# Four products of the first feed-forward block written ahead of a pair's scales

## The chip, the cores and the metric

One core of a Trainium2 chip runs the kernel. The metric is the device time of one execution in microseconds; for several runs the median is given. Beside it stands one profiled execution, from which all rows below come.

## The reference

Attention in which a query sees only the keys of its own cluster, and then a feed-forward block with a maximum of three products. Inputs: q, k, v of 4 batches x 8 heads x 768 tokens x 64, centroids of 8 heads x 16 x 64, three weights of 512 x 768 and one of 768 x 512.

```python
q_assign = np.argmax(np.einsum('bhsd,hcd->bhsc', q_n, c_n), axis=-1)
k_assign = np.argmax(np.einsum('bhsd,hcd->bhsc', k_n, c_n), axis=-1)
mask = q_assign[:, :, :, None] == k_assign[:, :, None, :]
scores = np.where(mask, scale * np.matmul(q, k.transpose(0, 1, 3, 2)), -1e9)
attn = softmax(scores)
x = np.matmul(attn, v)            # then tokens x 512
h = np.maximum(np.maximum(x @ w1, x @ w2), x @ w3)
out = h @ w_out
```

## The kernel before

Attention goes by heads, 32 in all, counted through the batches (head 8 is the first of batch 1), and by pairs of heads: pair (1,1) is the second pair of batch 1, heads 10 and 11. The tokens of a head are sorted by cluster. For each pair, `load_rows` (L591) loads rows of q, k and v into one of five `rows` buffers each; `sums` (L603 on ScalarE, L607 on VectorE) takes squares and the largest value; `scales` makes powers of two from them: small operations (L614 to L618), three matmuls that spread them over the partitions into a buffer called `one` (L623), a reduction (L628), a reciprocal (L631). `split_kv` and `split_q` (L657, L671 on ScalarE, L658, L672 on VectorE) write each row as two half-precision numbers. `scatter` (L692, GpSimd) sends key and value rows to their sorted places in memory, `read_back` fetches them in order (L727, L730). `order_q` sorts the queries with one-hot matrices (L747 on VectorE, L749 on TensorE). `scores` is matmuls (L784 to L791), a maximum (L795), exponentials (L800) and two half-precision parts (L804, L805), which a DMA transposes; `values` (L825 to L830) multiplies them with v, into a `one` buffer. Outputs go back to token order by a gather (L848) and are split and transposed for the feed-forward block (`x_split`); the last two heads of batch 0 are turned by matmuls on the spot instead (`turn`, L874 to L887).

The feed-forward block of a batch has 36 first products and 6 second ones. A first product (`hidden(jt, i)`) is twelve matmuls (L940) into a `one` buffer and one evacuation: a copy on ScalarE for i = 0 (L950), a running maximum on VectorE for i = 1, 2 (L952). After i = 2 a cast on ScalarE (L956) and a subtraction on VectorE (L957) make the two parts of h. In batch 0 the products of the two halves of the tokens alternate by three: products 0 to 2 are those of the first half with the first 128 columns, products 3 to 5 those of the second half. The first 9 matmuls of a product need x of pairs 0 to 2, the last three that of pair 3, which `turn` of head 7 finishes. The second products (`outp`, L973) take h and the output weights. The weights of products 18 to 35 are loaded and converted meanwhile (L287, then L292 on ScalarE, L294 on VectorE).

Two things set the order of the work. `put(at, p, u)` notes that piece u is written down in round `at`, at place p within it; rounds go by heads. The same p becomes the priority of its instructions (`at_prio`): the kernel is built with a scheduler that lays out the instructions of every engine ahead of time, each as soon as it can go, the lower p first. Buffers of one name, however, go round in the order in which the pieces are written down: there are two `one` buffers (`ps_one`), shared by `scales`, `values`, `hidden`, `outp` and a step of the weight scales (L257). `when(p, k)` moves pieces of batch 1 on by up to 2 heads, so `scales` of pair (1,1) stands at 7.6 in round 8, that of pair (1,2) at 9.1 in round 9, and `turn` of head 7 at 7.55 in round 8. `spread` puts the 42 units of batch 0's block evenly between 9.05 and 16: product 0 at 9.05 in round 9, product 1 at 9.2, then one every 0.165. `values` of head 8 ends round 9, behind product 5.

Of the kernel before, what the change touches and what calls it, by code (L numbers as in the profile page):

```python
# [23 lines left out]
def sorted_attn__then__maxout_ffn(  # L24
# [18 lines left out]
    B, H, D, S = qk.shape  # L43
# [724 lines left out]
    def turned(b, h):  # L768
        return b == 0 and h >= H - 2
# [138 lines left out]
    def split_after(b, pr):  # L908
        k = b * H + 2 * pr + 5
        return k if pr < NPAIR - 2 and k < B * H else None  # L910
# [98 lines left out]
        verdict.append(nc.values_load(bad, min_val=0, max_val=1))  # L1009


    plan = {}

    def put(at, p, u, *args):
        plan.setdefault(int(at), []).append((p, u, args))

    def spread(units, first, last, late=0):
        for i, u in enumerate(units):
            k = first + i * (last - first) / len(units)
            put(min(max(k, 0), B * H), k + late, u)  # L1020


    AHEAD = 2.0

    def when(p, k):
        return p + AHEAD * max(0.0, 1.0 - (k - H) / H) if k >= H else p

    for i in range(NRING):
        put(0, -4.95 + 0.01 * i, clear_ring, i)
    for b in range(B):  # L1030
        for hf in range(2):
            k = b * H + 4 * hf
# [9 lines left out]
        for pr in range(NPAIR):  # L1042
            u = pair_units(b, pr)
            k = b * H + 2 * pr
# [9 lines left out]
            for h in range(2):  # L1054
                put(max(k + h - 4, at), when(k + h - 3.85, k), u["split_kv"][h])
                at, p = max(k + h - 2, 0), when(k + h - 2.5, k)
                if H <= k + h < H + 4:
                    at, p = H + 1, max(p, H + 0.7)
                put(at, p, u["scatter"][h])
                for n, x in enumerate(u["read"][h]):  # L1060
                    p = when(k + h - 1.5, k) if not n or k + h >= H else k + h - 0.95
# [3 lines left out]
    for b in range(B):  # L1065
        for h in range(H):
            k = b * H + h
            put(H + 1 if k == H else k, when(k, k), scores, b, h)
            put(k + 1, when(k + 0.5, k) if k >= H - 1 else k + 1.2, values, b, h)
            if turned(b, h):  # L1070
                put(3, 3.5 + 0.1 * h, token_places, b, h)
                put(k + 1, k + 1.25 if k < H - 1 else when(k + 0.55, k), turn, b, h)
            else:
                put(min(k + 1 + LATE + (k + 5 < H), B * H), when(k + 0.6 + LATE + (k + 5 < H), k), gather, b, h)
        put(b * H + 3, b * H + 2.6, x_scale, b)
        for pr in range(NPAIR):
            k = split_after(b, pr)
            if turned(b, 2 * pr):
                continue
            if not b and pr == 2:  # L1080
                put(H - 1, H - 0.7, x_split, b, pr)
            elif k is not None:
                put(k + 2 * (not (b or pr)), when(k, k) + 0.01, x_split, b, pr)
            else:
                k = b * H + 2 * pr + 2 + LATE
                if k <= B * H:
                    put(k, when(k - 0.35, k - 1 - LATE), x_split, b, pr)
        if b + 1 < B:
            k = b * H + H + LATE
            units = [ffn_units(b, gi) for gi in range(NG)]  # L1090
            hid = [x[: 3 * JT] for x in units]
            if b:
                hid = [u for x in hid for u in x]
            else:
                hid = [u for jt in range(JT) for x in hid for u in x[3 * jt : 3 * jt + 3]]
            units = hid + [u for x in units for u in x[3 * JT :]]
            spread(units, k + 0.05, k + H, 0)
    put(B * H, B * H - 0.5, judge)
    spread(w_units(range(JT // 2)), 1, 6, 1)
    spread(w_units(range(JT // 2, JT)), 9, 11.5, 0)  # L1100
    spread(wo_units(), 11.5, 14, 0)

    def at_prio(p, u, *args):
        tc.cur_priority = 100000 + int(p * 1000)
        u(*args)

    at_prio(-12, lambda: centroids(load_centroids()))
    for k in range(B * H + 1):
        for p, u, a in sorted(plan.pop(k, []), key=lambda x: x[0]):
            at_prio(p, u, *a)  # L1110
    assert not plan, sorted(plan)
    at_prio(B * H, x_split, B - 1, NPAIR - 1)
    for gi in range(NG):
        for u in ffn_units(B - 1, gi):
# [745 lines left out]
```

## Time and profile before

| | |
|---|---|
| median of three runs | 754.81 us (749.6 to 756.33) |
| profiled execution | 751.73 us, span of its instructions 750.0 us |
| TensorE matmuls busy | 620.3 us, 83% of the span |
| VectorE busy | 489.4 us, 65% |
| ScalarE busy | 419.8 us, 56% |
| GpSimd busy | 407.7 us, 54% |
| mean granted TensorE clock | 0.917 |

Shares over the whole span say little here, since the limits change on the way: the attention of batch 0 alone until some 165 us, then attention with feed-forward blocks between, and the last block alone from 647 us on. The rows below therefore go by stretches and by the time line around 165 to 212 us. In a time line an entry has its start and its length in us; an "idle" in brackets is the time its engine had nothing to run just before it, and what ended that.

### The profile page before, as it was taken

What the parts mean: (1) busy time and instruction counts of PE and PEld (TensorE: products, weight loads), DVE (VectorE), ACT (ScalarE), POOL (GpSimd) and SP (SyncE); (2) the same over time, 40 slices, a digit from 0 to 9 for tenths busy, and PEclk for the clock granted to TensorE, in tenths of its full rate; (3) what the DMA queues carried; (4) which work ended last, traced back from release to release, by engine and by line L of the source; (5) the groups of instructions that cost most, each with busy time, mean ns of one, the idle gap of its engine ahead of it and who ended that gap; (6) DMA issues with size and microseconds to landing.
All of it is one profiled execution on the core that took longest, in us unless ns stands there. A gap on an engine that the chain in (4) does not pass through costs nothing.

```text
span 750.0 us, 12895 instructions
## 1 busy us (share of the span) xinstructions
PE 620.3 (83%) x4333; PEld 336.3 (45%) x4333; DVE 489.4 (65%) x1229; ACT 419.8 (56%) x1011; POOL 407.7 (54%) x426
## 2 busy tenths in 40 slices
PE   3556466467889887799999989979989999999995
PEld 1223233233445453354455545534545654564552
DVE  5898867779888999896769787835565522121230
ACT  5348978725879775665758577735556512211111
POOL 4576677735553777576755787746657545000000
PEclk8677777568899999999999999999999999999998
DMA  8865998799894995598776668576536644200001
GB/s 321 280 179 129 263 199 174 149 245 341 211 314 94 243 311 124 128 228 187 171 145 177 125 161 158 134 160 155 130 80 146 131 89 115 69 1 29 15 1 46
DMA packets 226907, 119.22 MB, mean 159 GB/s; under 512 B 196560, under 2 KB 205776, under 8 KB 226832
## 3 DMA queue, kind: packets, MB, share of 16 engines
q1 hardware_dynamic: 214928, 99.80, 54.3%
q0 software_dynamic: 11904, 18.50, 9.2%
q8 instruction: 36, 0.59, 0.3%
q14 instruction: 39, 0.32, 0.1%
HBM read 58.36 MB, written 28.84 MB: 116 GB/s over the span
## 4 chain that ended last, share of the span: by engine, by line
PE 46%; DMA 15%; DVE 12%; ACT 10%; issue 8%; POOL 6%; SPq 1%; DVEq 0%; POOLq 0%; ACTq 0%
PE one L940 24%; PE one L973 12%; PE big L749 4%; POOL kv L692 4%; DMA pt<-hl 4%; ACT e L800 3%; POOL xb L848 3%; DMA rows<-in_v_dram 2%; DMA xb<-o,cl_idx 2%; DVE hot L747 2%; DMA rows<-in_kr_dram 2%; DMA kv<-kv,cl_idx 2%; DVE kv L658 1%; DMA o<-of 1%; PE big L788 1%
## 5 line engine op out<-in xcount | busy, mean ns | idle before, releaser
L940 PE MATMUL one<-x,w 128*128 128x384 f16 x1728 | 296.5, 328 | 9.1 <-ACT wf_h L950 3.7
L692 POOL DMA_INDIRECT kv<-kv,cl_idx x192 | 207.0, 1078 | 116.1 <-issue 55.2
L848 POOL DMA_INDIRECT xb<-o,cl_idx x180 | 191.4, 1063 | 114.7 <-DMA o<-of 59.6
L940 PEld LDWEIGHTS <-w 128*128 128x128 f16 x1728 | 167.7, 98 | 123.7 <-issue 15.3
L749 PE MATMUL big<-hot,q 128*128 128x512 f16 x384 | 113.4, 410 | 31.6 <-DVE hot L747 19.3
L800 ACT ACTIVATE e<-big,nm,sc_al 128x128 f32<-128x128 f32 x256 | 113.4, 462 | 42.2 <-DVE nm L796 27.4
L747 DVE TENSOR_SCALAR hot<-line,cl_code 128x1024 f16<-128x1024 f16 x192 | 93.0, 504 | 8.3 <-PE big L749 8.1
L749 PEld LDWEIGHTS <-q 128*128 128x128 f16 x384 | 36.6, 102 | 76.8 <-issue 47.3
L952 DVE SCALAR_TENSOR_TENSOR wf_h<-one,wf_h 128x384 f32<-128x384 f32 x48 | 26.5, 552 | 54.0 <-PE one L940 53.9
L952 DVE SCALAR_TENSOR_TENSOR vf_h<-one,vf_h 128x384 f32<-128x384 f32 x48 | 26.5, 552 | 46.5 <-PE one L940 42.8
L973 PE MATMUL one<-wo,vf_h 128*128 128x512 f16 x216 | 49.8, 387 | 7.0 <-ACT o L982 6.4
L800 ACT ACTIVATION_READ_ACCUMULATOR e<-big,nm,sc_al 128x1 f32 x256 | 53.6, 209 | 0.0
L973 PE MATMUL one<-wo,wf_h 128*128 128x512 f16 x216 | 48.6, 379 | 1.4 <-ACT o L982 1.4
L825 PE MATMUL one<-vt,pt 128*128 128x64 f16 x256 | 29.2, 202 | 16.0 <-DMA pt<-hl 14.9
L757 ACT CAST qt<-big 128x1024 f16<-128x1024 f32 x32 | 32.3, 1010 | 17.7 <-PE big L749 17.3
L805 DVE SCALAR_TENSOR_TENSOR hl<-e,hl 128x1024 f16<-128x1024 f32 x32 | 39.0, 1218 | 3.3 <-ACT hl L804 3.1
L982 ACT ACTIVATE o<-one,so 128x512 f32<-128x512 f32 x24 | 16.1, 683 | 43.3 <-PE one L973 41.1
L795 DVE TENSOR_REDUCE nm<-big 128x8 f32<-128x1024 f32 x32 | 38.9, 1215 | 1.8 <-PE big L791 1.7
L658 DVE SCALAR_TENSOR_TENSOR kv<-rows,sc_s,kv 128x384 f16<-128x384 f32 x64 | 37.3, 612 | 3.3 <-ACT kv L657 3.1
L956 ACT CAST wf_h<-wf_h 128x384 f16<-128x384 f32 x24 | 12.3, 514 | 48.0 <-DVE wf_h L952 47.9
L956 ACT CAST vf_h<-vf_h 128x384 f16<-128x384 f32 x24 | 12.3, 513 | 43.6 <-DVE vf_h L952 43.6
L657 ACT ACTIVATE kv<-rows,sc_s 128x384 f16<-128x384 f32 x64 | 35.7, 610 | 1.6 <-DVE sc_s L631 1.5
(242 smaller groups left out, 925.6 us busy)
## 6 DMA issues: line engine op xcount, KB each, us to landing
stage<-in_qk_dram SPq DMA_DIRECT2D x32, 384.0 KB, 7.2
wd<-in_moe_w_dram SPq DMA_DIRECT2D x18, 512.0 KB, 5.7
vt<-kv SPq DMA_DIRECT2D x32, 256.0 KB, 3.7
o<-of SPq DMA_DIRECT2D x30, 256.0 KB, 3.5
rows<-in_qr_dram SPq DMA_DIRECT2D x16, 384.0 KB, 5.2
rows<-in_kr_dram SPq DMA_DIRECT2D x16, 384.0 KB
rows<-in_v_dram SPq DMA_DIRECT2D x16, 384.0 KB, 3.4
out_dram<-o SPq DMA_DIRECT2D x24, 256.0 KB, 2.8
```

The lines of the kernel that those rows point to most:

```text
L657: d["kv_hi", h] = nc.scalar.activation(kv[:, :, at], x, AF.Copy, scale=s[:, i : i + 1])
L658: d["kv_lo", h] = nc.vector.scalar_tensor_tensor(kv[:, :, at + 1], x, s[:, i : i + 1], kv[:, :, at], op0=ALU.mult, op1=ALU.subtract)
L692: i = nc.gpsimd.indirect_dma_start(out=ring[at], out_offset=bass.IndirectOffsetOnAxis(ap=index(h, n, 1), axis=0), in_=d["kv", h][:, n].rea ...
L747: nc.vector.tensor_scalar(a, line, code, None, op0=ALU.is_equal)
L749: nc.tensor.matmul(t[:, lo : lo + 512], d["q16"][:, h * QT + n].rearrange("p a d -> p (a d)"), a[:, lo : lo + 512], start=(n == 0), stop=( ...
L795: d["max", i] = nc.vector.tensor_reduce(nm, ts, axis=AX.X, op=ALU.max)
L800: nc.scalar.activation(x[:, j], ts[:, j], AF.Exp, bias=nm[:, j : j + 1], scale=d["al"], accum_out=sm[:, j : j + 1])
L805: d["lo", i] = nc.vector.scalar_tensor_tensor(hl[:, 1], x, 2.0**14, hl[:, 0], op0=ALU.mult, op1=ALU.subtract)
L848: d["back", i] = nc.gpsimd.indirect_dma_start(out=d["x"][:, n, i * D : i * D + D], out_offset=None, in_=od, in_offset=bass.IndirectOffsetO ...
L940: nc.tensor.matmul(t[:, 0:NB], w16[:, jt, wa, i, ct], x16[b, ct][:, xa * QT + gi * G : xa * QT + (gi + 1) * G, :], start=(n == 0), stop=(n ...
L952: nc.vector.scalar_tensor_tensor(m, t[:, 0:NB], 2.0**-23, ms[jt], op0=ALU.mult, op1=ALU.max)
L973: nc.tensor.matmul(t[:, 0:DM], h16[jt][:, ha, tt * P : (tt + 1) * P], wo16[:, jt, wa, :], start=(n == 0), stop=(n == 3 * JT - 1),)
```

## The change

The first four units of batch 0's block, products 0 to 3, are written down in round 8 at 7.56, right behind `turn` of head 7 (7.55) and ahead of `scales` of pair (1,1) (7.6). Their priorities stay 9.05 and up, since they are called through `at_prio` with the p of the place they had. The other 38 units keep place and priority. `at_prio` itself only moves up in the file.

```diff
+    def at_prio(p, u, *args):
+        tc.cur_priority = 100000 + int(p * 1000)
+        u(*args)
+
     plan = {}
@@
     AHEAD = 2.0
+    NFIRST = 4
@@
             units = hid + [u for x in units for u in x[3 * JT :]]
-            spread(units, k + 0.05, k + H, 0)
+            if b:
+                spread(units, k + 0.05, k + H, 0)
+            else:
+                p0, n_units = k + 0.05, len(units)
+                p_unit = (H - 0.05) / n_units
+                for i in range(NFIRST):
+                    put(H, H - 0.44 + 0.001 * i, at_prio, p0 + i * p_unit, units[i])
+                spread(units[NFIRST:], p0 + NFIRST * p_unit, k + H, 0)
@@
-    def at_prio(p, u, *args):
-        tc.cur_priority = 100000 + int(p * 1000)
-        u(*args)
```

## Rows read from the trace of the kernel before

**Rows 1.** Busy time by stretches: us busy (instructions), then TensorE's clock, DMA.

```profile
172.00:194.00 22.00, 14.77 (x83) 6.39 (x79) 19.11 (x51) 12.96 (x32) 15.92 (x16) 0.72 1.07 340
194.00:212.00 18.00, 17.22 (x117) 9.33 (x116) 17.43 (x45) 11.31 (x19) 10.89 (x10) 0.96 0.83 242
212.00:342.00 130.00, 109.24 (x854) 61.46 (x853) 119.43 (x340) 97.57 (x244) 83.89 (x78) 0.97 0.75 197
342.00:743.00 401.00, 383.17 (x2642) 212.36 (x2640) 202.61 (x444) 186.11 (x458) 191.25 (x181) 1.00 0.50 111
```

**Rows 2.** Time line of TensorE, 168 to 195 us: start, us, instruction, [idle before].

```profile
168.64 1.62 PE L940 MATMUL one<-x,w 128*128 128x384 f16 x9
...
171.01 0.65 PE L940 MATMUL one<-x,w 128*128 128x384 f16 x3
...
193.59 0.48 PE L623 MATMUL one<-ident,sc 128*128 128x128 bf16 x3
193.86 1.49 PE L940 MATMUL one<-x,w 128*128 128x384 f16 x4
```

**Rows 3.** Time line of TensorE, 202 to 212 us.

```profile
202.21 2.11 PE L940 MATMUL one<-x,w 128*128 128x384 f16 x12 [0.78 <-DVE vf_h L952]
...
206.54 4.08 PE L940 MATMUL one<-x,w 128*128 128x384 f16 x24
...
211.97 0.19 PE L825 MATMUL one<-vt,pt 128*128 128x64 f16 x1
```

**Rows 4.** Time line of VectorE (DVE), 166 to 193 us.

```profile
166.66 0.56 DVE L628 TENSOR_REDUCE pall<-one 128x3 f32<-128x384 f32 x1
...
167.66 0.18 DVE L631 RECIPROCAL sc_s<-pall 128x3 f32<-128x3 f32 x1
...
172.61 0.61 DVE L658 SCALAR_TENSOR_TENSOR kv<-rows,sc_s,kv 128x384 f16<-128x384 f32 x1
...
175.03 1.01 DVE L672 SCALAR_TENSOR_TENSOR q<-rows,sc_s,q 128x768 f16<-128x768 f32 x1
...
183.21 0.95 DVE L607 TENSOR_REDUCE sc<-rows 128x1 f32<-128x768 f32 x1 [0.91 <-DMA rows<-in_v_dram]
...
192.96 0.17 DVE L617 TENSOR_SCALAR sc<-sc 128x2 f32<-128x2 f32 x1 [1.27 <-ACT q L603]
```

**Rows 5.** Time line of ScalarE (ACT), 169 to 192 us.

```profile
169.65 2.13 ACT L657 ACTIVATE kv<-rows,sc_s 128x384 f16<-128x384 f32 x4
...
174.29 0.49 ACT L950 ACTIVATE vf_h<-one 128x384 f32<-128x384 f32 x1
...
187.45 0.46 ACT L800 ACTIVATE e<-big,nm,sc_al 128x128 f32<-128x128 f32 x1 [3.12 <-DVE nm L796]
...
191.15 0.86 ACT L603 ACTIVATE q<-rows 128x768 bf16<-128x768 f32 x1
```

**Rows 6.** Time line of GpSimd (POOL): first scatters of heads 9, 10 and 12.

```profile
173.50 0.98 POOL L692 DMA_INDIRECT kv<-kv,cl_idx  x1 [11.98 <-DVE kv L658]
...
182.20 0.98 POOL L692 DMA_INDIRECT kv<-kv,cl_idx  x1 [0.30 <-DVE cl_oh L468]
...
201.97 0.98 POOL L692 DMA_INDIRECT kv<-kv,cl_idx  x1 [4.67 <-DVE kv L658]
```

**Rows 7.** Time line of SyncE's DMA queue (SPq): the V rows, a weight load.

```profile
176.07 0.33 SPq L591 DMA_DIRECT2D rows<-in_v_dram  x1
...
178.69 2.75 SPq L287 DMA_DIRECT2D wd<-in_moe_w_dram  x2
```

**Rows 8.** Groups by line: count | busy us, mean ns | idle before, releasers.

```profile
L940 PE MATMUL one<-x,w 128*128 128x384 f16 x1728 | 296.5, 328 | 9.1 <-ACT wf_h L950 3.7 <-DVE of L830 1.9 <-DVE vf_h L952 1.8
L952 DVE SCALAR_TENSOR_TENSOR vf_h<-one,vf_h 128x384 f32<-128x384 f32 x48 | 26.5, 552 | 46.5 <-PE one L940 42.8 <-issue 3.6
L957 DVE TENSOR_TENSOR vf_h<-vf_h 128x384 f16<-128x384 f32 x24 | 13.2, 550 | 4.6 <-ACT vf_h L956 4.6
L950 ACT ACTIVATE vf_h<-one 128x384 f32<-128x384 f32 x24 | 11.8, 493 | 12.6 <-PE one L940 12.6
```

## The prediction

> **What bounds the kernel now.** I read the busy time of the engines by stretches first [rows 1], then TensorE's timeline where the change acts [rows 2, 3], then those of VectorE, ScalarE, GpSimd and the DMA queue of SyncE in the same stretch [rows 4 to 7], and last the groups of one product's instructions [rows 8].
>
> [...] From 342 to 743 us TensorE is busy 383.17 of 401 us: there it is the bound. From 194 to 342 VectorE is: 17.43 of 18 us and then 119.43 of 130, with TensorE at 17.22 of 18 and 109.24 of 130. [...]
>
> [...] Product 0 of the first FFN runs at 168.64 (nine matmuls) and 171.01 (the three that need head 7) [rows 2]. Product 1 needs nothing that product 0 did not have, and starts at 193.86, 22 us later, right behind the three matmuls of the scales of pair (1,2) at 193.59 [rows 2]. Both write a `one` buffer; there are two, and they go round as written: scales (1,1), product 0, scales (1,2), product 1. Those scales are late because the pair's rows are: the V rows are issued at 176.07 [rows 7], VectorE takes them at 183.21 after waiting 0.91 us for them, the squares follow on ScalarE at 191.15 [rows 5], and the small operation behind these stands at 192.96 [rows 4].
>
> **The change, part by part.** Nothing is computed more or less, and no DMA is added. Products 0 to 3 keep their priorities (9.05 and up, the last rank there) and go ahead of scales (1,1) and scales (1,2) in the round of `one` buffers. SyncE's and GpSimd's queues are not written to differently; they move only where what they wait for moves.
>
> *Taken out of 194 to 212.* Products 1, 2 and 3. Twenty-four matmuls take 4.08 us at 206.54 [rows 3], so one product is 2.04 us and three are 6.1 us of TensorE. On VectorE two maxima of 0.552 and one subtraction of 0.550 [rows 8] make 1.65 us; on ScalarE there is one copy of 0.493 [rows 8] and one cast. VectorE is full there and TensorE nearly, so the lower bound of the gain is 0 (the wait for head 8's transposed weights, which `values` uses at 211.97 [rows 3], stays where it is), and the upper bound the 6.1 us. I take VectorE's 1.65 us: the weight conversions and key splits that the next heads wait for stand in its queue between those maxima. Most of TensorE's 6.1 us has no taker: products 4 and 5 may come at 194 instead of 206.54, but product 6 is written behind `values` of head 8.
>
> *Put into 168 to 182.* The same 6.1 and 1.65 us. From 172 to 194 TensorE idles 22 - 14.77 = 7.2 us and VectorE 22 - 19.11 = 2.9 us [rows 1]. It fits, so I cost it at nothing; this idle time is its cover, and without it VectorE would pay the 1.65 us again.
>
> *Scales (1,1) later.* Their matmuls now need the buffer that product 2 frees. Product 0 ends about 171.7; its copy, held back on ScalarE to 174.29 today behind the pair's own splits [rows 5], could come at 172.2; product 2 ends 2.04 us later, its maximum 0.55 after that: 174.8 at the earliest. Other matmuls and higher-ranked VectorE work get between, so I take 177, against 166.66 for the reduction that ends them today [rows 4]: about 10 us late. What is late next:
> - The pair's splits, on ScalarE from 169.65 [rows 5] and on VectorE to 176.04 (175.03 and 1.01 for q [rows 4]). GpSimd is released for head 9 at 173.50 after 11.98 us of waiting and takes head 10 at 182.20 [rows 6]. Head 10's splits would be done near 177 + 1.2 (from the reduction to the end of the reciprocal at 167.84 [rows 4]) + 0.5 on ScalarE (2.13 us for four [rows 5]) + 2 x 0.6 on VectorE = 180; cost 0. If the scales take until 180, some 1 us; and GpSimd has a pause of 4.67 us in front of 201.97 [rows 6] that swallows it.
> - The V rows of (1,2) need a buffer that the q split frees: 176.07 becomes about 182. On VectorE they came 7.1 us after issue (183.21), so about 189. The next use is the small operation at 192.96, held by the squares at 191.15 [rows 4, 5]. About 3 us are left: cost 0, but thin. Behind them on SyncE stands a weight load at 178.69 [rows 7], 512 KB for a conversion on ScalarE and VectorE; if it stays behind, it is up to 6 us late.
> - In exchange VectorE is rid of the pair's five splits (4 x 0.6 + 1.0 = 3.4 us) between 170 and 177, when head 8's one-hots wait for it; ScalarE waits 3.12 us for that head's maximum at 187.45 [rows 5]. The splits come back some us later, in front of head 9. I count it as 0, with bounds of 3.4 us either way.
>
> [...]
>
> *The sum.* 0 - 1.65 + 0 + about 0.5 for the thin covers = -1.2 us. After 212 the shift passes through: VectorE is full to 342 and TensorE from there. The profiled execution took 751.73 us (span 750.0), so it would be 750.5. The median of the three runs shown is 754.81, which is 3.1 above that execution; I put the forecast between the two, at 752.5 us.
>
> **The rivals.**
> 1. *Slower: the scales take the place of the wait.* They carry rank 7.6, but now hang on products of rank 9.05 to 9.4, which give way to everything. For it: VectorE has only 2.9 us free in 172 to 194 [rows 1], and rows, scales and splits of (1,2) come after one another. Against it: three covers (4.67 us at GpSimd, 3 us at the V rows, the idle TensorE). It decides from a reduction at 180 on; each us more then costs one. If the scales come at 184 and VectorE stands at the V rows, the delay of 176.07 is 13 us, less 3 to 4 of cover: +9 us, 763.
> 2. *Faster: the lead is kept.* If the first FFN stays three products ahead to its end at 342, TensorE has 6.1 us less to do in the stretch that it bounds: 752.5 - 4.9 = 747.6, as 1.2 of the 6.1 is counted. [...] Against it: every later product stays written between the same `values` and scales, so a lead waits at the first of them, at 211.97. [...]
> 3. *The plan moves.* The order on every queue is planned again by priorities from the moved buffers on, so some other stall among the 570 us behind may open or close. A VectorE wait for one late load is worth some 7 us (176.07 to 183.21), of either sign: 745 or 760. No row tells which.
>
> **How the numbers follow.** Forecast 0.45, first rival 0.20, second 0.25, third 0.10, half to each side. The likeliest case alone spans 747.5 to 758 (the 3.4 us of the splits, the 4.7 and 3 us of the covers and the spread of the runs). To leave out no more than 2 in 10 the range takes in the second rival with part of the clock (741) and the first with its 9 us (764). A change of under 1%, about 7.5 us, can hardly be told from none in this kernel. Faster by over 1% takes the second rival nearly whole and half of the third: 0.29. Slower takes most of the first and half of the third: 0.23. Within 1%: 0.48.
>
> **What would show it.** Products 0 to 3 end before 182, and product 4, no longer product 1, follows the matmuls of scales (1,2). The reduction of scales (1,1) stands near 177. Head 10's scatter starts near 182 and that of head 12 near 202; the V rows of (1,2) are issued near 182 and VectorE does not stand for them. `Values` of head 8 comes at 210 to 212 and the first FFN's first output near 341. The prediction is wrong if the reduction comes after 180 and GpSimd or VectorE shows a new wait of some us, or if the stretch from 342 on begins with fewer products left.

## The result and the profile after

The changed kernel takes 761.10 us (median of 9 runs, 758.27 to 765.27) beside 753.73 for the kernel before (9 runs, 749.48 to 756.33): a ratio of 1.0103, 95% interval 1.0074 to 1.0132. It is slower, by 1%. Ratios, here and below, are formed from runs in the faster of two states alone; times are medians of all runs. Its profiled execution took 765.27 us (span 763.5, mean granted clock 0.909). That is 4 us above its own median, and the one of before lies 2 us below its median, so differences between these two traces overstate the loss.

The four stretches of [rows 1], in the changed kernel:

```profile
172.00:194.00 22.00, 16.29 (x116) 8.23 (x114) 16.32 (x42) 11.71 (x19) 0.00 (x0) 1.00 0.69 225
194.00:212.00 18.00, 13.55 (x73) 6.55 (x73) 15.58 (x50) 15.76 (x37) 13.63 (x12) 0.72 0.83 251
212.00:342.00 130.00, 107.18 (x824) 58.97 (x825) 117.78 (x324) 89.72 (x220) 94.11 (x84) 0.92 0.84 205
342.00:743.00 401.00, 381.96 (x2634) 211.48 (x2632) 208.66 (x471) 190.79 (x477) 201.28 (x187) 0.99 0.51 113
```

The early stretch is fuller (TensorE 16.29 us, before 14.77) and its granted clock is 1.00 (before 0.72). But the hole has only moved: from 194 to 212 TensorE is busy 13.55 us instead of 17.22 at 0.72 instead of 0.96, and GpSimd stands still from 172 to 194.

TensorE (start, length, instruction, idle before it), to be read beside [rows 2, 3]:

```profile
169.61 3.67 PE L940 MATMUL one<-x,w 128*128 128x384 f16 x17
...
182.17 0.98 PE L940 MATMUL one<-x,w 128*128 128x384 f16 x5
183.41 0.33 PE L623 MATMUL one<-ident,sc 128*128 128x128 bf16 x3 [0.26 <-DVE vf_h L952]
...
205.95 4.06 PE L940 MATMUL one<-x,w 128*128 128x384 f16 x24
```

Products 0 to 3 end at 183.15. The three matmuls behind them are those of the scales of pair (1,1), which the kernel before had done by 166.66 [rows 4]. Product 4 starts at 205.95, where it stood before (206.54 [rows 3]). ScalarE, VectorE and GpSimd in the same time:

```profile
175.27 0.78 ACT L292 CAST top<-wd 128x512 f16<-128x512 bf16 x1 [3.43 <-DMA wd<-in_moe_w_dram]
175.92 0.49 ACT L950 ACTIVATE vf_h<-one 128x384 f32<-128x384 f32 x1
...
191.27 2.13 ACT L657 ACTIVATE kv<-rows,sc_s 128x384 f16<-128x384 f32 x4 [1.53 <-DVE sc_s L631]
```

```profile
182.19 0.69 DVE L294 SCALAR_TENSOR_TENSOR w<-wd,top 128x512 int32<-128x512 int32 x1 [3.10 <-ACT top L292]
182.80 0.55 DVE L952 SCALAR_TENSOR_TENSOR vf_h<-one,vf_h 128x384 f32<-128x384 f32 x1
...
186.80 0.54 DVE L628 TENSOR_REDUCE pall<-one 128x3 f32<-128x384 f32 x1
...
191.07 0.17 DVE L631 RECIPROCAL sc_s<-pall 128x3 f32<-128x3 f32 x1
```

```profile
194.94 1.11 POOL L692 DMA_INDIRECT kv<-kv,cl_idx  x1 [33.31 <-DVE kv L658]
...
203.95 0.98 POOL L692 DMA_INDIRECT kv<-kv,cl_idx  x1 [0.30 <-DVE hot L747]
```

Read as a chain: product 0's copy (175.92) stands behind a weight cast that waited 3.43 us for its load; product 2's maximum (182.80) stands behind a weight conversion that waited 3.10 us for the cast; only then is the buffer free for the scales. The reduction comes at 186.80 (166.66 in [rows 4]), the first key split at 191.27 (169.65 in [rows 5]), and GpSimd's first scatter for head 9 at 194.94 after 33.31 us without work (173.50 after 11.98 in [rows 6]). In these two rows a later instruction of ScalarE and of VectorE did stand behind one that waited, 3.43 and 3.10 us.

### The profile page after: what moved, and what is told of

It reads as the page before. It is cut to its first block, busy times and chain, and to the rows that moved or that the text cites. A ratio compares the mean times of both kernels' runs of the same rounds, so it can differ in the third digit from the quotient of the medians.

```text
span 763.5 us, 12868 instructions
## 1 busy us (share of the span) xinstructions
PE 626.1 (82%) x4333; PEld 337.1 (44%) x4333; DVE 488.0 (64%) x1229; ACT 420.2 (55%) x1011; POOL 415.6 (54%) x426
## 4 chain that ended last, share of the span: by engine, by line
PE 33%; issue 18%; DMA 16%; DVE 12%; POOL 11%; ACT 8%; SPq 1%; POOLq 0%; DVEq 0%; ACTq 0%
PE one L940 20%; PE one L973 6%; POOL kv L692 6%; DMA pt<-hl 5%; POOL xb L848 5%; ACT e L800 4%; DMA kv<-kv,cl_idx 3%; DMA xb<-o,cl_idx 3%; PE big L749 2%; DVE hot L747 2%; DMA o<-of 1%; DMA rows<-in_v_dram 1%; DVE nm L795 1%; DMA rows<-in_kr_dram 1%; DVE kv L658 1%
## 5 line engine op out<-in xcount | busy, mean ns | idle before, releaser
L940 PE MATMUL one<-x,w 128*128 128x384 f16 x1728 | 300.1, 331 | 11.2 <-ACT o L982 3.9
L692 POOL DMA_INDIRECT kv<-kv,cl_idx x192 | 213.0, 1109 | 120.5 <-issue 57.2
L848 POOL DMA_INDIRECT xb<-o,cl_idx x180 | 193.4, 1074 | 116.6 <-DMA o<-of 61.1
L940 PEld LDWEIGHTS <-w 128*128 128x128 f16 x1728 | 168.6, 99 | 128.3 <-issue 21.2
L749 PE MATMUL big<-hot,q 128*128 128x512 f16 x384 | 115.4, 416 | 29.2 <-DVE hot L747 14.3
L747 DVE TENSOR_SCALAR hot<-line,cl_code 128x1024 f16<-128x1024 f16 x192 | 90.8, 492 | 11.0 <-PE big L749 10.3
L749 PEld LDWEIGHTS <-q 128*128 128x128 f16 x384 | 36.6, 103 | 72.0 <-issue 42.0
L952 DVE SCALAR_TENSOR_TENSOR wf_h<-one,wf_h 128x384 f32<-128x384 f32 x48 | 26.6, 555 | 58.9 <-PE one L940 57.2
L952 DVE SCALAR_TENSOR_TENSOR vf_h<-one,vf_h 128x384 f32<-128x384 f32 x48 | 26.6, 554 | 47.3 <-PE one L940 44.7
L973 PE MATMUL one<-wo,vf_h 128*128 128x512 f16 x216 | 48.4, 379 | 4.3 <-DVE of L830 1.7
L973 PE MATMUL one<-wo,wf_h 128*128 128x512 f16 x216 | 48.2, 379 | 1.4 <-ACT o L982 1.4
L825 PEld LDWEIGHTS <-pt 128*128 128x128 f16 x256 | 24.9, 104 | 27.9 <-DMA pt<-hl 26.2
```

The source lines that it names most:

```text
L692: i = nc.gpsimd.indirect_dma_start(out=ring[at], out_offset=bass.IndirectOffsetOnAxis(ap=index(h, n, 1), axis=0), in_=d["kv", h][:, n].rea ...
L747: nc.vector.tensor_scalar(a, line, code, None, op0=ALU.is_equal)
L749: nc.tensor.matmul(t[:, lo : lo + 512], d["q16"][:, h * QT + n].rearrange("p a d -> p (a d)"), a[:, lo : lo + 512], start=(n == 0), stop=( ...
L825: nc.tensor.matmul(o[:, j], pt[:, j], v[:, j, 0], start=True, stop=False)
L848: d["back", i] = nc.gpsimd.indirect_dma_start(out=d["x"][:, n, i * D : i * D + D], out_offset=None, in_=od, in_offset=bass.IndirectOffsetO ...
L940: nc.tensor.matmul(t[:, 0:NB], w16[:, jt, wa, i, ct], x16[b, ct][:, xa * QT + gi * G : xa * QT + (gi + 1) * G, :], start=(n == 0), stop=(n ...
```

## The experiments

Two theories were to be told apart. **A, the buffer:** the scales of (1,1) wait for the `one` buffer that product 2 frees, so heads 9 to 12 come late. **C, the order:** the planner, finding other times early on, lays out the work of the later rounds differently, and that order is worse. A third, **B**, was crowding: the products take ScalarE and VectorE from more urgent work.

**First series.** It fell on a chip on which the kernel before itself took 935.19 us (median), so its ratios stand only beside one another. The edits, each against the changed kernel but the third, which is against the kernel before:

```diff
e1 and f1, products behind scales (1,1)
-                    put(H, H - 0.44 + 0.001 * i, at_prio, p0 + i * p_unit, units[i])
+                    put(H, H - 0.39 + 0.001 * i, at_prio, p0 + i * p_unit, units[i])
e2, f2 (on the change) and e3 (on before), head 9's key split one round earlier
-                put(max(k + h - 4, at), when(k + h - 3.85, k), u["split_kv"][h])
+                put(H if k + h == H + 1 else max(k + h - 4, at), when(k + h - 3.85, k), u["split_kv"][h])
e4 and f4, scales (1,1) in a `big` buffer
-            a = one()
+            a = big() if g == NPAIR + 1 else one()
```

> The four products are written at 7.61, behind the scales of pair (1,1) and still ahead of those of pair (1,2). Theory A (buffers: the scales wait for the `one` buffer that product 2 frees, the key splits of heads 10 and 9 wait for the scales, GpSimd waits for them): the reduction of scales (1,1) is back near 167, the first scatter of head 9 near 173.5 instead of 194.9, the products stay early (before 185), and the time is 0.993 to 1.002 of before. Theory B (crowding: the products' evacuations between 169 and 185 stand in the queues of ScalarE and VectorE among weight conversions and delay what is behind them): 1.006 to 1.012, as in the change. Theory C (the new plan happens to be worse somewhere behind 300 us): scatter of head 9 near 173.5 and still 1.005 or more.

> The change, and in it the key split of head 9 is written ahead of that of head 10 (round 8 instead of 9, same priority), so that its `kv16` buffer comes first in the round. Theory A: the reduction of scales (1,1) stays near 187, but head 9's scatter no longer waits for it and starts by 174, GpSimd waits for head 10 until about 194 instead; head 9's maximum comes back from 214 towards 206, and half or more of the loss goes: 1.000 to 1.006. Theories B and C: nothing that they name is touched, 1.008 to 1.013.

> The kernel before, with the key split of head 9 written ahead of that of head 10 and nothing else; the control for e2. If `kv16` is what held head 9's split (all theories allow it), the split runs before 160 and head 9's scatter follows head 8's at about 162 instead of 173.5. Time 0.995 to 1.002 of before if head 9's keys were not the bound; down to 0.985 if the 12 us of GpSimd's wait were on the path.

> The change, with the matmuls of scales (1,1) going to a buffer of the `big` round (shared by turn, query sort and scores) instead of `one`: the products stay written ahead of the scales, but no longer hold their buffer. Theory A: reduction near 168 to 172, head 9's scatter near 174 to 178, time 0.993 to 1.004. Theory B: products still in the way, 1.006 to 1.012.

Measured: 1.015 (1.0067 to 1.0233) for e1, 1.0068 (1.0024 to 1.0112) for e2, 0.9956 (0.99 to 1.0012) for e3, 0.9976 (0.9929 to 1.0023) for e4. Both e1 and e4 take the wait of A away, and by these ratios they disagree. But the executions of one kernel spread widely there (before: 913.74 to 948.94 us), and by the medians of all runs e1 is at 1.0025 and e4 at 1.0008 (937.51 and 935.97 us), so the series doesn't decide. Three of the edits therefore went to a chip with the usual time; the change itself took the place of e3.

**Second series** (before: 754.74 us).

> The change itself, unaltered, as the measure beside the others of this series. All theories: reduction of scales (1,1) 18 to 22 us later than in the kernel before, first scatter of head 9 as much later, 1.007 to 1.013 of before where a chip runs the kernel before near 754 us. The series of e1 to e4 ran where the kernel before took 935 us, so its ratios are set beside this run's only if this chip does the same.

> As e1: products behind scales (1,1), ahead of (1,2). Theory A (buffers): reduction back at 167, head 9's scatter near 173.5, products still before 185; 0.993 to 1.002. Theory B (crowding by the products' evacuations): 1.006 to 1.012. Theory C (chance of the plan behind 300 us): scatter back and still 1.005 or more.

> As e2: the change with head 9's key split written ahead of head 10's. Theory A: scales stay late, head 9's scatter does not; 1.000 to 1.006. Theories B and C: 1.008 to 1.013.

> As e4: the change with the matmuls of scales (1,1) in a `big` buffer. Theory A: reduction near 168 to 172, scatter near 174 to 178, 0.993 to 1.004. Theory B: 1.006 to 1.012.

Measured: f0 1.0116 (1.0047 to 1.0185), f1 1.0188 (1.0122 to 1.0255), f2 1.0197 (1.0126 to 1.0269), f4 1.0202 (1.0132 to 1.0272). GpSimd in f1, then in f2:

```profile
173.84 1.10 POOL L692 DMA_INDIRECT kv<-kv,cl_idx  x1 [11.77 <-DVE kv L658]
```

```profile
162.59 2.46 POOL L692 DMA_INDIRECT kv<-kv,cl_idx  x1 [0.30 <-issue]
...
192.64 1.65 POOL L692 DMA_INDIRECT kv<-kv,cl_idx  x1 [21.18 <-DVE s_tmp L493]
```

In f1 head 9 is back at its old time, and the first block's first output at 342.48 (before 342.2), and yet the kernel loses 1.9%. So A can't be the whole cause. In f2 head 9 waits for nothing, head 10 comes at 192.64, and the kernel loses 2.0%, more than any of my theories allowed; all of that loss lies early (first output at 355.56). What f1, f4 and the change have in common lies later, in the stretch from the second block's first product to its first output. Busy time in it, for before, after and f1 (columns as in [rows 1]):

```profile
375.20:487.60 112.40, 109.19 (x846) 63.19 (x845) 88.74 (x215) 78.66 (x211) 80.28 (x74) 1.00 0.68 150
```

```profile
381.90:505.50 123.60, 117.44 (x870) 65.89 (x870) 91.76 (x233) 77.43 (x201) 86.30 (x77) 0.97 0.64 140
```

```profile
382.70:507.20 124.50, 115.11 (x857) 64.55 (x856) 90.11 (x218) 76.58 (x201) 82.42 (x77) 0.97 0.66 139
```

The stretch grows from 112.4 to 123.6 and 124.5 us. It holds 11 to 24 more matmuls, most of them from the sorting by clusters of batch 3's first half (its matmul L532), which in the change falls into it and in f1 begins at its edge, at 382.26. In before, then after:

```profile
362.50 0.38 PE L532 MATMUL four<-cl_oh,before 128*128 128x512 f16 x1
```

```profile
405.88 0.38 PE L532 MATMUL four<-cl_oh,before 128*128 128x512 f16 x1
```

**Third series: the order held fast.** For each engine a chain of edges without a semaphore gives the planner the order of the instructions written down from round 16 on. No instruction is added.

```diff
+            for k in memoryview(raw).cast("h")[at : at + n]:
+                x = late[k]
+                if prev is not None:
+                    tc.add_manual_dep(
+                        x, prev.name,
+                        mybir.DependencyInfo(mybir.DependencyClass.NoSync, mybir.DependencyReason.DATA),
+                        reason="pinned order",
+                    )
+                prev = x
```

> The change as it is, up to round 16 of the plan; everything that is written down from round 16 on (the work behind about 300 us) goes into each engine's queue in the order that the kernel before has. Theory C (most of the loss is the other order that the planner gives the later work): the stretch from the second FFN's first product 1 to its first output falls back from 123.6 to 112 to 115 us, only the early loss of 4 to 5 us up to the first FFN's outputs stays, ratio 1.003 to 1.008. Rival (the loss behind 375 us comes from the work arriving late, whatever its order): that stretch stays at 120 to 125 us and the ratio at 1.010 to 1.016.

> The kernel before up to round 16 of the plan, with nothing of the change in it; everything written down from round 16 on stands in each engine's queue in the order that the changed kernel has. Theory C: the first FFN's first output stays near 342 us, as before; the stretch from the second FFN's first product 1 to its first output grows from 112.4 to 120 to 125 us; ratio 1.008 to 1.016, with no product of the first FFN moved at all. Rival (lateness, not order): 0.997 to 1.004, that stretch at 112 to 115 us.

> The four products behind the scales of batch 1's first pair, so that these scales and the scatter of head 9 come as early as before, and the later work in the order of the kernel before. Theories A and C together: neither the early loss nor the late one, the first output at 340 to 344 us, the second FFN's stretch at 112 to 115 us, ratio 0.994 to 1.003. If one of them is false, a loss stays: 1.006 or more; a stretch still above 120 us would say that the order isn't what the late loss hangs on.

> The kernel before with one step moved: head 9's key split is written down one round earlier, ahead of head 10's; the later work in the order of the kernel before. A: head 9's scatter follows head 8's at once, 8 to 11 us earlier than in the kernel before, and head 10's comes later; the first output at 340 to 343 us and the ratio at 0.993 to 1.002. If the later heads need head 10's V rows more than head 9's, the first output comes later than 344 us and the ratio is 1.004 or more.

Measured beside 753.87: x1 764.96, 1.018 (1.0109 to 1.0251); x2 766.10, 1.018 (1.0121 to 1.0239); x3 756.24, 1.0033 (1.0001 to 1.0065); x4 755.98, 1.0033 (1.0003 to 1.0062). x2 has nothing of the change in it but the later order, and loses 1.8%, somewhat more than I expected; in its trace the queues of ScalarE, VectorE and SyncE leave before's order only from 309 us on. Its first output comes at 347.98, not near 342. Its stretch and its cluster matmul (L616 there, 84 lines further down) are those of after:

```profile
383.80:507.50 123.70, 117.09 (x870) 65.50 (x870) 91.69 (x233) 77.36 (x201) 85.41 (x78) 0.97 0.64 142
```

```profile
406.24 0.38 PE L616 MATMUL four<-cl_oh,before 128*128 128x512 f16 x1
```

So C is true by itself. But x1, with the wait and the old later order, missed my 1.003 to 1.008: its stretch is back at 113.8 us as expected, and it loses 1.8% all the same. x3, without either, loses next to nothing (0.3%, the edge of what I expected). x4 shows that releasing GpSimd for head 9 eleven us earlier (162.52) gains nothing in the kernel before; its first output comes at 346.58, and later than 344 was to be the sign that the later heads need head 10's V rows more than head 9's.

**Fourth series: the wait alone.** In x1 the rounds 9 to 15 had been planned anew. Here everything from round 9 on keeps before's order, the four products aside; y4 differs from y1 in the scales' buffer alone (the edit of e4). y2 is the edit of e1 under the same order. y5 is the kernel before with the scales of pair (1,2) in a `big` buffer (`g == NPAIR + 2`; 128 x 1024 f32 in the program, called four-bank in the expectations), which frees product 1 without moving it, later order as in before.

> The four products stand as in the change; everything else that is written down from round 9 of the plan on (from about 190 us) goes into each engine's queue in the order of the kernel before. So the scales of batch 1's first pair still wait for product 2's buffer, but no other order of the work follows. If the wait for the buffer alone is enough: first scatter of head 9 at 190 to 196 us, first output at 346 us or later, ratio 1.008 to 1.020, like the run that pinned only the work from round 16 on. If the loss hangs on the planner's other order of the cluster parts of batches 2 and 3 alone: 0.997 to 1.005.

> The kernel of the run beside it, with one thing other: the scales of batch 1's first pair take their bank from the four-bank buffers (big) and not from the two one-bank buffers (one) that the products fill. Neither the wait for the buffer nor another order is left of the change. Theory (these two are the whole loss): the reduction of these scales is back at 166 to 170 us, head 9's first scatter at 172 to 177 us, ratio 0.995 to 1.004. If a loss of 1.008 or more stays, the products themselves do harm where they stand.

> The four products written down behind the scales of batch 1's first pair instead of ahead of them, everything else from round 9 on in the order of the kernel before. The other way to take away the wait for the buffer. Same theory: ratio 0.995 to 1.004, first output at 340 to 344 us. Rival: the products are worth something once they cost no wait: below 0.995.

> The kernel before, without the change, in which the scales of batch 1's second pair, which hold product 1 until 193.86 us there, take a four-bank buffer; the work from round 16 on in the order of the kernel before. If a free product 1 is worth the 20 us of idle TensorE that it has ahead of it, the first output comes 3 us or more earlier (339 us or less) and the ratio is 0.990 to 0.997. If the first FFN's end is set by VectorE and the heads' chain (the reading of the stage 194 to 342 us), product 1 starts by 175 us and the ratio stays at 0.997 to 1.005.

Measured beside 755.78: y1 766.63, 1.0152 (1.0098 to 1.0205); y4 755.10, 0.9999 (0.9964 to 1.0035); y2 757.01, 1.0030 (1.0001 to 1.0059); y5 763.92, 1.0107 (1.0056 to 1.0158). The lines of y1 and y4 lie 123 further down than those of the changed kernel: L751 is the reduction L628, L815 the scatter L692, L1075 the maximum L952, L872 the matmul L749, L1063 the product L940, L1096 the output L973, and L730 the take-up of V rows, L607. y1, VectorE, GpSimd, TensorE:

```profile
175.83 0.56 DVE L1075 SCALAR_TENSOR_TENSOR vf_h<-one,vf_h 128x384 f32<-128x384 f32 x1 [0.20 <-ACT vf_h L1073]
...
179.81 0.56 DVE L1075 SCALAR_TENSOR_TENSOR vf_h<-one,vf_h 128x384 f32<-128x384 f32 x1 [1.46 <-PE one L1063]
...
182.79 0.56 DVE L751 TENSOR_REDUCE pall<-one 128x3 f32<-128x384 f32 x1 [0.17 <-PE one L746]
...
196.91 0.95 DVE L730 TENSOR_REDUCE sc<-rows 128x1 f32<-128x768 f32 x1 [2.39 <-DMA rows<-in_v_dram]
```

```profile
187.24 1.10 POOL L815 DMA_INDIRECT kv<-kv,cl_idx  x1 [26.09 <-DVE kv L781]
...
215.06 0.98 POOL L815 DMA_INDIRECT kv<-kv,cl_idx  x1 [4.10 <-DVE kv L781]
```

```profile
357.16 1.03 PE L1096 MATMUL one<-wo,vf_h 128*128 128x512 f16 x4
```

The same three of y4:

```profile
167.78 0.56 DVE L751 TENSOR_REDUCE pall<-big 128x3 f32<-128x384 f32 x1
...
184.21 0.95 DVE L730 TENSOR_REDUCE sc<-rows 128x1 f32<-128x768 f32 x1 [0.38 <-DMA rows<-in_v_dram]
```

```profile
174.04 1.10 POOL L815 DMA_INDIRECT kv<-kv,cl_idx  x1 [12.46 <-DVE kv L781]
...
204.20 0.98 POOL L815 DMA_INDIRECT kv<-kv,cl_idx  x1 [4.50 <-DVE kv L781]
```

```profile
344.29 1.03 PE L1096 MATMUL one<-wo,vf_h 128*128 128x512 f16 x4
```

One buffer is the only difference in the program, and in the traces the queues of GpSimd and SyncE have the same order, those of ScalarE and VectorE another one only between 168 and 195 us. With the wait the reduction is 15.0 us later, head 9's scatter 13.2, the take-up of the next pair's V rows 12.7, head 12's scatter (the later of the two GpSimd rows) 10.9, the first output 12.9, and the kernel 11.5 by the medians (766.63 - 755.10): most of the wait goes through to the end when no order changes. y4 also answers B: the products and their evacuations stand in the same stretch, and nothing is lost.

Both causes can be laid side by side, by TensorE's time line of each trace (us):

| kernel | wait for the buffer | order of the later work | product 0 to second block's first product | from there to the end |
|---|---|---|---|---|
| before | no | before's | 206.6 | 367.3 |
| y4 | no | before's | 207.3 | 368.1 |
| y1 | yes | before's | 220.7 | 368.8 |
| f2 | yes, but not for head 9 | planned anew | 221.3 | 368.4 |
| x2 | no | the change's | 212.6 | 373.8 |
| f1 | no | planned anew | 212.8 | 376.4 |
| after | yes | the change's | 212.3 | 374.9 |

Under before's order the wait costs 13 to 14 us of the first part and next to nothing of the second; f2 loses as much, and as early, though head 9 is free there. The other order (x2, f1, after) costs some 6 us of the first part and 6 to 9 of the second, with or without the wait. Together they cost no more than the order alone (after against x2 and f1); that the planner moved other work into the time of the wait would explain it, but no run shows it. So either cause is enough for a loss, and they don't add up: by the medians the change loses 7.4 us (761.10 - 753.73), x2 12.2 and y1 10.9. How the change's 7.4 us divide between the two isn't shown.

Three things stay open. Whether the wait reaches the end through GpSimd's scatters of heads 10 and 11 or through the next pair's V rows wasn't tried apart; f2 and x4 only exclude head 9's scatter. Which piece of the other order costs most wasn't tried apart: the cluster parts of batch 3 take turns at buffers with their neighbours, and can't be moved alone. And y5's loss (I had expected at most 1.005), where rounds 9 to 15 are planned anew too, was not taken apart; its row of the first scatter of head 12 (215.66, before 201.97 [rows 6]) says only that the heads come late there as well.

## Why the prediction was wrong

It said 752.5 us, no change; the chip said 761.1. That this still lies inside the range, which reached to 764, is in part luck: the upper end stood for the first rival's wait, and the planner's other order, which has no part in that rival, is enough for the loss by itself. By its own steps:

- *Put into 168 to 182, costed at nothing.* Right. y4 has the four products there, the rest within 2.5 us of its old times, and a ratio of 0.9999.
- *Taken out of 194 to 212, 1.65 us gained, up to 6.1.* No gain came: y4's interval reaches from 2.7 us faster to 2.6 us slower, and y2 and x3, which have the products early too, are at 1.0030 and 1.0033. The stretches 172 to 194 and 194 to 212 of y4:

```profile
172.00:194.00 22.00, 16.46 (x116) 8.43 (x115) 20.34 (x52) 13.20 (x32) 15.99 (x14) 1.00 1.03 318
194.00:212.00 18.00, 13.67 (x77) 5.68 (x76) 15.35 (x39) 12.92 (x22) 10.76 (x11) 0.72 0.86 216
```

  Nothing moves up into the place that products 1 to 3 leave. TensorE waits there for the one-hots of the next heads, and product 4 starts at 209.01, behind them, where the order held fast puts it. In x3, where the planner was free up to round 16, product 4 starts at 202.26 (206.54 before [rows 3]), and nothing is gained either. y4:

```profile
204.37 1.01 PE L872 MATMUL big<-hot,q 128*128 128x512 f16 x2 [2.20 <-DVE hot L870]
...
209.01 4.07 PE L1063 MATMUL one<-x,w 128*128 128x384 f16 x24
```

  The prediction put the idle time before product 1 down to the `one` buffers, which "go round as written". That was half of it: the order held product 1, but where the products come early without the wait, nothing behind them does (first output at 344.29 in y4, 342.10 in y2, 344.03 in x3, 342.16 before). The second rival (faster, the lead kept) falls with it. The range's lower end, 741, counts in part of a gain from the clock, and no run shows such a gain: in y4 the granted clock is 1.00 instead of 0.72 from 172 to 194, but 0.72 instead of 0.96 from 194 to 212, and the ratio is 0.9999.
- *Scales (1,1) later, near 177.* Too small: 186.80 in the changed kernel, 182.79 in y1, so 16 to 20 us late and not 10. I had let products 0, 1 and 2 follow one another at 2.04 us with free evacuations. In y1 the maxima of products 1 and 2 came at 175.83 and 179.81, and the scales' matmuls stood behind those of product 3 at 182.43; in the changed kernel two weight conversions that wait for a load stood in front of the evacuations as well, and with other work of VectorE between them the reduction started 3.4 us after its matmuls and the reciprocal 4.3 us after that (1.0 in [rows 4]).
- *What is late next: each consequence put at 0, and 0.5 us for thin covers.* This is the step that failed: y1 against y4 measure 11.5 us for it. Three covers were wrong.
  - GpSimd's release for head 9 was left at 173.50; in y1 it is 187.24. Head 9 belongs to pair (1,0), but its split is written down in round 9, behind that of head 10 in round 8. Moving that place alone frees its scatter (162.59 in f2, 162.52 in x4); that the round of the three `kv16` buffers is what ties the two is my reading of the program and not shown. But f2 and x4 also say that head 9 alone isn't worth much either way.
  - The V rows of (1,2) were to be issued at 182 instead of 176.07, with 3 us to spare. In y1 they are issued at 188.90, and VectorE takes them at 196.91 after standing 2.39 us for them (183.21 after 0.91 in [rows 4]). In f2 they are issued at 193.47, and it loses 14.7 us of the first part, as y1 does (14.1).
  - The pause of 4.67 us in front of head 12's scatter was to swallow a delay. It is still there: 4.10 us in y1, 4.50 in y4. What releases head 12 came late as well, so the pause covered next to nothing.
- *After 212 the shift passes through.* For the wait alone this held (y1 against y4: 12.9 us at the first output, 11.5 at the end). For the change it left out a term: the planner's other order, the third rival with a chance of 0.10 and 7 us, costs 12.2 us when alone (x2), and f1, without the wait, loses 13.1.
- *The first rival,* "the scales take the place of the wait", deciding from a reduction at 180 on and at 763 us, is what y1 shows: a reduction at 182.79, V rows issued 12.8 us late (the rival said 13), VectorE standing for them, and 766.63 us. Its chance of 0.20 was held down by three covers. The idle TensorE did take the products (y4), but the pause at GpSimd and the 3 us at the V rows did not hold. The sign of its test was right: the reduction came after 180, and GpSimd and VectorE had longer waits.

One size in the description of the kernel is off, and no step above hangs on it: `spread` runs from 9.05 to 17, so the units stand 7.95 / 42 = 0.19 apart, not 0.165.

## What to carry to other kernels

Before a piece is written down earlier, list every buffer it takes and every later writer of the same name: it puts itself ahead of them in the round, however low its priority, and an urgent piece then waits for a leisurely one. A buffer of another kind for the urgent piece tells whether that is the cost, but only with the order held fast: f4 without that lost 2.0%, y4 with it nothing. For where a planner lays out the queues, a small edit comes with a new order far behind it; holding the old order fast separates the edit from its echo, which here were of the same size.

## What the runs showed of the hardware

The same program took 935.19 us on one chip and 753 to 756 on the others. GpSimd's gathers there, in the kernel before with head 9's split moved (the first row; the second is the kernel before on a usual chip), are no longer in themselves (mean 1042 and 1063 ns), but wait 166.5 instead of 59.6 us for the stores that they follow. These are not the only longer waits there, and why that chip is slower stays open:

```profile
L848 POOL DMA_INDIRECT xb<-o,cl_idx x180 | 187.6, 1042 | 264.7 <-DMA o<-of 166.5 <-issue 47.4 <-DVE nm L796 20.9
```

```profile
L848 POOL DMA_INDIRECT xb<-o,cl_idx x180 | 191.4, 1063 | 114.7 <-DMA o<-of 59.6 <-issue 48.8 <-DVE xh L300 4.4
```

So the verdict on one edit can differ by chip: scales (1,1) in a `big` buffer are at 0.9976 (0.9929 to 1.0023) there, as e4, and at 1.0202 (1.0132 to 1.0272) on a usual one, as f4.
